# The prologue of a three-stage kernel laid out anew: loads four ahead, batch 0's attention beside the weight fold, block 0 fed from SBUF

## The chip, the cores and the metric

The kernel runs on one core of one Trainium2 chip. The metric is the device time of one execution in microseconds (us), from a few runs. A core has a matrix engine (TensorE, PE in the profile), a vector engine (VectorE, DVE), a scalar engine (ScalarE, ACT), GpSimd (POOL), and SyncE (SP), which here issues nearly all transfers. Each engine works through its own instructions in order and waits on semaphores that others raise. SBUF is the core's working memory, PSUM the memory that TensorE writes.

## The reference

Attention over keys and values that are averaged in groups of eight, then two feed-forward layers. B = 8 batches, H = 8 heads, S = 576 positions, D = 64, so 4608 tokens of 512 features. The second layer's inner width is 2048, the first's 1024.

```python
k_p = k.reshape(B, H, Sp, pool, D).mean(axis=3)
v_p = v.reshape(B, H, Sp, pool, D).mean(axis=3)
scores = scale * np.matmul(q, k_p.transpose(0, 1, 3, 2))
scores = scores - np.max(scores, axis=-1, keepdims=True)
attn = np.exp(scores)
attn = attn / (np.sum(attn, axis=-1, keepdims=True) + 1e-09)
attn_out = np.matmul(attn, v_p)
x = attn_out.transpose(0, 2, 1, 3).reshape(B * S, H * D)
x = ((x @ w1) * (x @ w2)) @ w3 @ w_out          # first layer
out = np.maximum(x @ w_in, 0.0) ** 2 @ w_out2   # second layer
```

The weights come as 64-bit floats, the rest as 32-bit floats.

## The kernel before, in words

Since `w3` and `w_out` of the first layer are multiplied with nothing between them, the kernel first makes W = w3 @ w_out (the **fold**), and then treats the tokens in nine **blocks** of 512. Block i needs a = x @ w1 and b = x @ w2 (`stage_ab`, eight steps u, 24 products of 128x512 each) and then (a*b) @ W (`stage_w`, 12 products a step, run two steps behind). So a block has 288 products, and 264 of block 0's fall before block 1 begins. After the blocks comes the second layer, which starts with the products of L965.

**Weights.** A weight tile of 128x512 arrives as 512 KB of raw 64-bit words. ScalarE makes two passes over it (`words`, L131 and L132) and VectorE three (`join`, L140, L141 and L143) to get 32-bit floats. Then w3 is turned on TensorE (L616) and copied back by ScalarE (L617), and w1 and w2 are split into a high part (ScalarE) and a low part (VectorE, L114), as each later product is made as high*high + high*low + low*high. The fold's own products are plain 32-bit ones (L641, two instructions each, 128 in all). There are 8 tiles of w_out, 16 of w3, 8 first halves of w1 and w2 (which stay in SBUF for `stage_ab`'s steps u < 4) and 8 second halves (steps u >= 4).

**Second halves.** `second_half` loads, converts and splits one of them, and stores its four pieces to DRAM (`store`, L207, 32 stores in all). Every block, block 0 too, fetches them again through a ring of eight buffers (`fetch`, L222; tiles `un`), two fetches for each w of each step u >= 4. Before step u = 3 of block 0 the kernel issues what is left of the second halves, then fills the ring. The quarter list (`make_quarters`: the second layer's weights, converted and stored to DRAM) starts only when the second halves are all issued, with one step of the list in three ticks.

**Attention.** `build_tasks` lists the attention of all batches as small tasks: transposes of k (`pe_kt`), scores with softmax (`pe_s`), transposes of the weights of attention (`pe_t`) and products with v (`pe_av`, which writes x, the block's input). A tick (`tick`) comes after each product of the fold, and after each six products of a block. Each tick adds `rate[0]` to a credit, and a whole credit runs a task: 0.7 a tick in the fold (from its twelfth product), 0.6 later. k and v are summed by VectorE from loads into `raw_p`, three buffers that the weights' raw tiles use too (`kv_parts`, L298). Once v is summed, `load_v` places it with 4 + 12 small transfers within SBUF (L333, L337). Block i waits until its tokens' `pe_av` are issued (`tokens_ready`): block 0 needs all of batch 0, block 1 all of batch 1.

**Order in the fold.** The first three w3 rows are folded together, with their first halves and the w_out tiles loaded into x's eight buffers (`x_p`), which stand empty then. All other raw tiles go through `raw_p`, each loaded just ahead of its conversion (`load64`, L125). From its fourth step on the attention starts: `load_k(0)`, `load_q(0, 0)`, and from the sixth `load_v(0)`. From its twelfth step on, a first half of w1 or w2 is converted at every fourth step (a step is one piece of 128 of the inner width, for all rows folded together).

## Time and profile before

| | us |
|---|---|
| median of 3 runs | 1585.99 |
| lowest, highest | 1585.23, 1586.9 |
| span of the profiled execution | 1583.2 |
| median above that span | 2.8 |

| engine | busy us in the span | share | instructions |
|---|---|---|---|
| PE | 1514.2 | 96% | 6944 |
| DVE | 992.7 | 63% | 1778 |
| ACT | 784.0 | 50% | 1905 |
| POOL | 83.9 | 5% | 146 |

The profile is of one execution; its own time beyond the span isn't listed, so the median stands for it. Busy time is the time with at least one instruction under way. PEclk is the granted TensorE clock as a share of full speed (2.4 GHz; the lower of its two levels, 1.2 GHz, is 0.5, and a stretch that has both shows a mean).

### The profile page before, as it was taken

The numbers are of one execution on the slowest core, as the hardware profiler recorded it, in microseconds if no ns is written. First come the engines' busy times: TensorE is split into PE (matmuls) and PEld (weight loads), VectorE is DVE, ScalarE is ACT, GpSimd is POOL, SyncE is SP. The second block draws the span as 40 slices with busy tenths as digits, with TensorE's granted clock in tenths as the row PEclk, the third lists the DMA queues.
The fourth block names the chain that finished last, engine by engine and source line by source line (L and its number), as shares of the span: only waits on it lengthen the run. The fifth ranks groups of instructions, "written<-read, shape, count | busy, mean of one in ns | idle before, by whom it ended". The sixth has DMA issues, their size and how long they took to land.

```text
span 1583.2 us, 21959 instructions
## 1 busy us (share of the span) xinstructions
PE 1514.2 (96%) x6944; PEld 1215.8 (77%) x6944; DVE 992.7 (63%) x1778; ACT 784.0 (50%) x1905; POOL 83.9 (5%) x146
## 2 busy tenths in 40 slices
PE   6788799998999999999999999999999999999998
PEld 3346577786868888887888887888788878888888
DVE  7688556675746667576435458648864877476542
ACT  6486544544425345555323565456445644464431
POOL 1111101110101010111000000000000000000000
PEclk8899799999989999999999999999999999999999
DMA  8455674756546676666727667677777766776774
GB/s 269 137 172 178 155 226 135 216 155 179 167 136 181 166 248 191 179 185 208 240 70 244 201 194 240 194 220 219 232 195 218 223 202 192 221 219 192 208 222 155
DMA packets 302930, 308.07 MB, mean 195 GB/s; under 512 B 131552, under 2 KB 188896, under 8 KB 302816
## 3 DMA queue, kind: packets, MB, share of 16 engines
q1 hardware_dynamic: 297632, 297.24, 64.4%
q10 hardware_dynamic: 5184, 9.44, 1.6%
q8 instruction: 56, 0.92, 0.2%
q14 instruction: 58, 0.48, 0.1%
HBM read 247.46 MB, written 56.62 MB: 192 GB/s over the span
## 4 chain that ended last, share of the span: by engine, by line
PE 78%; DVE 10%; DMA 4%; ACT 4%; SPq 3%; issue 2%; DVEq 0%; ACTq 0%
PE ps_w L183 23%; PE o L1052 14%; PE acc L183 11%; PE ps_a L965 5%; PE ps_c L965 5%; PE ps_d L965 5%; PE o L1112 3%; PE ps_h L183 3%; PE ps_b L965 2%; DVE gs L1030 2%; PE ps_s L414 2%; DVE gt L114 2%; PE ps_av L183 1%; DMA raw<-in_moe_w_dram 1%; PE ps_w L641 1%
## 5 line engine op out<-in xcount | busy, mean ns | idle before, releaser
L1052 PE MATMUL o<-gt,un 128*128 128x512 f32 x1344 | 330.8, 390 | 4.9 <-DVE gt L114 4.5
L1052 PEld LDWEIGHTS o<-gt,un 128*128 128x128 f32 x1344 | 251.3, 188 | 61.2 <-DVE gt L114 9.0
L114 DVE TENSOR_TENSOR gt<-gs,gt 128x512 fp32r<-128x512 f32 x240 | 163.8, 687 | 186.2 <-ACT gt L113 185.9
L113 ACT CAST gt<-gs 128x512 fp32r<-128x512 f32 x240 | 148.5, 619 | 164.0 <-PE o L1052 111.2
L183 PE MATMUL ps_w<-x,wt 128*128 128x512 f32 x864 | 221.6, 401 | 1.5 <-DVE x L495 0.8
L183 PE MATMUL acc<-gt,Wt 128*128 128x512 f32 x864 | 218.8, 396 | 0.0
L183 PE MATMUL ps_w<-x,un 128*128 128x512 f32 x864 | 216.2, 401 | 2.0 <-DVE x L495 1.5
L183 PEld LDWEIGHTS ps_w<-x,un 128*128 128x128 f32 x864 | 162.7, 192 | 36.1 <-DMA un<-u_w 2.0
L183 PEld LDWEIGHTS ps_w<-x,wt 128*128 128x128 f32 x864 | 157.9, 189 | 34.8 <-DVE x L495 2.1
L183 PEld LDWEIGHTS acc<-gt,Wt 128*128 128x128 f32 x864 | 158.2, 188 | 32.0 <-issue 1.0
L431 ACT ACTIVATE att<-ps_s,mx 128x72 f32<-128x72 f32 (+1 forms) x320 | 98.2, 320 | 76.6 <-DVE mx L429 70.3
L972 ACT ACTIVATE r<-r 128x512 f32<-128x512 f32 x96 | 60.5, 631 | 112.6 <-DVE r L1002 111.9
L965 PE MATMUL ps_c<-x2o,un 128*128 128x512 f32 x384 | 97.7, 390 | 0.0
L965 PE MATMUL ps_d<-x2o,un 128*128 128x512 f32 x384 | 97.4, 389 | 0.0
L965 PE MATMUL ps_a<-x2o,un 128*128 128x512 f32 x384 | 97.4, 389 | 0.0
L694 DVE TENSOR_TENSOR gf<-asb,ps_w 128x512 f32<-128x512 f32 x72 | 49.3, 685 | 71.3 <-PE ps_w L183 68.9
L973 ACT ACTIVATE gs<-r 128x512 f32<-128x512 f32 x144 | 89.5, 629 | 1.6
L1030 DVE TENSOR_TENSOR gs<-gs 128x512 f32<-128x512 f32 x128 | 83.6, 683 | 2.0 <-ACT gs L973 0.7
L690 ACT COPY asb<-ps_w 128x512 f32<-128x512 f32 x72 | 42.5, 590 | 84.6 <-PE ps_w L183 80.1
L965 PEld LDWEIGHTS ps_c<-x2o,un 128*128 128x128 f32 x384 | 71.9, 188 | 15.7 <-DVE u L996 0.9
L965 PEld LDWEIGHTS ps_d<-x2o,un 128*128 128x128 f32 x384 | 72.1, 188 | 15.0
L965 PEld LDWEIGHTS ps_a<-x2o,un 128*128 128x128 f32 x384 | 72.1, 188 | 15.0
(109 smaller groups left out, 1973.6 us busy)
## 6 DMA issues: line engine op xcount, KB each, us to landing
un<-u_w SPq DMA_DIRECT2D x144, 256.0 KB
un<-u_A SPq DMA_DIRECT2D x128, 256.0 KB
un<-u_S SPq DMA_DIRECT2D x128, 256.0 KB
un<-u_oA SPq DMA_DIRECT2D x128, 256.0 KB
un<-u_oS SPq DMA_DIRECT2D x128, 256.0 KB
raw<-in_moe_w_dram SPq DMA_DIRECT2D x32, 512.0 KB
raw<-in_moe_w_out_dram SPq DMA_DIRECT2D x24, 512.0 KB
x2d<-st ACTq DMA_DIRECT2D x36, 256.0 KB
```

The costliest lines, as they stand in the source:

```text
L113: nc.scalar.copy(hi, src)
L114: (eng or nc.vector).tensor_sub(lo, src, f32(hi))
L183: (lambda a=a, b=b, i=i: nc.tensor.matmul(ps, a, b, start=first and i == 0, stop=last and i == n - 1))
L431: nc.scalar.activation(av[:, h0 + h], sv[:, h], ACTF.Exp, bias=mx[:n, h:h + 1], scale=scale, accum_out=sm[:n, h0 + h:h0 + h + 1])
L690: nc.scalar.copy(asb, ps)
L694: nc.vector.tensor_mul(gf, asb, pss[1])
L965: nc.tensor.matmul(ps, l, r, start=first and j == 0, stop=j == len(todo) - 1, skip_group_check=True)
L972: nc.scalar.activation(t, src, ACTF.Relu)
L973: nc.scalar.activation(take(name), t, ACTF.Square)
L1030: nc.vector.tensor_sub(src, a, src)
L1052: nc.tensor.matmul(ob[x][o], l, r, start=u == 0 and m != 5 and j == 0, stop=u == NU - 1 and j == 2, skip_group_check=True)
L1112: nc.tensor.matmul(acc[o][:, y * PC:(y + 1) * PC], l, r, start=u == 0 and y == 0 and j == 0, stop=u == U2 - 1 and j == 2, skip_group_check ...
```

## The change

- A new pool `sec_p` (four tiles of 4 KB a partition) takes the place of the ring until block 0 has ended; the ring is then allocated where `sec_p` lay.
- The fold's conversions stand in one list, sorted by a position at which each begins: five positions ahead of its use at the latest, at least two apart (one apart ahead of the first product), w1's and w2's first halves at every sixth position from 14 on. Each conversion's passes stand at successive positions. At the pass `act` of conversion n the load of conversion n + 4 is issued (`PRE`), into `x_p` until the first x tile exists, then into `sec_p`.
- k of batch 0 is loaded first of all, into W's buffers, v's first three tiles too, and q of batch 0 into the buffers of w1 and w2; their sums and transposes become attention tasks. Batch 1's k and v loads are held until position 44.
- Credit per tick: 1.4 ahead of the first product, 0.85 from there, 0.5 from position 48, 0.7 in blocks 0 and 1, 0.6 later. The fold has 73 positions, with a tick each: six ahead of its first product, 64 with a product and three behind.
- `second_half` begins after the fold, one step a tick, w1 and w2 in turns. It writes to four tiles of `sec_p` and four of `prep_p`; block 0 reads them there. The 32 stores are still made, five ticks after the split, for blocks 1 to 8. The quarter list begins when the ring exists, after block 0.

```diff
 LEAD = 3
+
+PRE = 4
+
+W12_AT = 14
+
+W12_GAP = 6
 
 LAG = 2
...
-    ring = ctx.enter_context(tc.tile_pool(name="ring", bufs=RING))
     wW_p = tc.alloc_tile_pool(name="wW", bufs=U1)
     w0_p = tc.alloc_tile_pool(name="w0", bufs=2 * KD)
     prep_p = tc.alloc_tile_pool(name="prep", bufs=4)
+    sec_p = tc.alloc_tile_pool(name="sec", bufs=4)
     at_p = tc.alloc_tile_pool(name="att", bufs=1, side="right")
 
 
...
-            n_raw[0] += 1
-        r = pool.tile([P, TB, 2], U32, tag="x" if pool is x_p else "raw", name="raw")
+    def early_pool():
+
+        return sec_p if xt else x_p
+
+    def load64(src, pool):
+
+        tag = "x" if pool is x_p else "w" if pool is prep_p else "raw"
+        r = pool.tile([P, TB, 2], U32, tag=tag, name="raw")
         nc.sync.dma_start(r, src.bitcast(U32).rearrange("p (c t) -> p c t", t=2))
         return r
 
...
     n_used = [0]
...
             nc.sync.dma_start(f32(r), unit(key))
             ahead.append(r)
 
...
     def load_back():
-        if back["kv"] and (not held[0] or len(back["kv"]) > 9):
+        if back["kv"] and not wait_kv[0] and (not held[0] or len(back["kv"]) > 9):
             back["kv"].pop(0)[1]()
         if back["q"] and ticks[0] % 2 == 0:
             back["q"].pop(0)[1]()
...
-            raws[j] = r = raw_p.tile([P, POOL, D], F32, tag="raw", name="kv")
+            pool, tag = (raw_p, "raw") if b else (wW_p, "w")
+            raws[j] = r = pool.tile([P, POOL, D], F32, tag=tag, name="kv")
...
+        if b == 0:
+            fits = NJ if src is k else U1 - NJ
+            for j in range(fits):
+                load(j)
+            rest = [lambda: [load(j) for j in range(fits, NJ)]]
+            return rest + [(lambda j=j: total(j)) for j in range(NJ)] + last
         parts = [(lambda j=j: part(j)) for j in range(NJ + 2)] + last
         what = (src is k, b)
-        if b:
-            back["kv"].extend((what, fn) for fn in parts)
-        else:
-            for fn in parts:
-                fn()
+        back["kv"].extend((what, fn) for fn in parts)
...
+    q_nat = {}
+
+    def turn_q(b, hf, i):
+
+        if (b, hf) not in qts:
+            qts[b, hf] = at_p.tile([P, NP, HW], F32, tag="qT", name="qT", bufs=2)
+        t = qts[b, hf]
+        s0 = QT[HALF[hf][0]][0]
+        s1, n = QT[i]
+        r = q_nat.pop((b, i))
+        ps = ps_at.tile([P, NP, P], F32, tag="at", name="ps_q")
+        for hp in range(NP):
+            nc.tensor.transpose(
+                ps[:, hp, :n], r[:n, 2 * hp:2 * hp + 2, :].rearrange("p h d -> p (h d)"),
+                ident[:n, :n])
+        nc.scalar.copy(t[:, :, s1 - s0:s1 - s0 + n], ps[:, :, :n])
+
...
+        if b < EARLY:
+            for i in HALF[hf]:
+                s1, n = QT[i]
+                if b == 0:
+                    if i % 2 == 0:
+                        q_nat["w"] = w0_p.tile([P, 2, H, D], F32, tag="w", name="q_nat")
+                    r = q_nat["w"][:, i % 2]
+                else:
+                    r = tmp_p.tile([P, H, D], F32, tag="cg", name="q_nat", bufs=3)
+                nc.sync.dma_start(r[:n], q[b, :, s1:s1 + n, :].rearrange("h p d -> p h d"))
+                q_nat[b, i] = r
+            return
...
+                put(lambda part=part: pe_kt(b, part), [("k", b)])
...
+        def turns(g):
+            b, i = divmod(g, len(QT))
+            for hf, tiles in enumerate(HALF):
+                if b < EARLY and i == tiles[0]:
+                    for x in tiles:
+                        put(lambda hf=hf, x=x: turn_q(b, hf, x))
+
+        def ahead_of(g):
+            b, i = divmod(g, len(QT))
+            at = (len(QT) if b + 1 < EARLY else HALF[1][0], len(QT))
+            early = b + 1 < EARLY
+            if i + 1 == at[0] and b + 1 < B:
+                put(lambda b=b: load_q(b + 1, 0))
+            if i + 1 == at[1] and b + 1 < B:
+                if not early:
+                    put(lambda b=b: load_q(b + 1, 1))
+                kt(b + 1)
+            if g + 1 < NG:
+                turns(g + 1)
+                sc(g + 1)
+            if i + 1 == at[1] and early:
+                put(lambda b=b: load_q(b + 1, 1))
...
+        for fn in first_k:
+            put(fn)
         kt(0)
+        turns(0)
         sc(0)
-        put(lambda: load_q(0, 1))
...
+            if g + 1 != len(QT):
+                ahead_of(g)
...
+            if g == 0:
+                for fn in first_v:
+                    put(fn)
...
+            if g + 1 == len(QT):
+                ahead_of(g)
...
+        mms = [(m, f) for m in range(nm) for f in range(LEAD)]
+        mms += [(m, f) for f in range(LEAD, U1) for m in range(nm)]
+        use = {}
+        for pos, (m, f) in enumerate(mms):
+            use.setdefault(("w3", f, m // nh), pos)
+            use.setdefault(("wo", m), pos)
+        begin = {}
+        nxt = len(mms)
+        for key, pos in sorted(use.items(), key=lambda z: -z[1]):
+            begin[key] = nxt = min(pos - 5, nxt - (2 if nxt > 1 else 1))
+        w12 = [("w12", n, kc) for kc in range(KD) for n in range(2)]
+        for j, key in enumerate(w12):
+            begin[key] = W12_AT + W12_GAP * j
+        convs = sorted(begin, key=lambda key: begin[key])
+        raws = {}
+        n_load = [0]
...
+                raws[key] = load64(src, early_pool())
+
+        def conv(n, key):
+            st = {}
+
+            def act():
+                load(n + PRE)
+                if key[0] == "w3":
...
+            steps = [act, lambda: join(raws.pop(key), st["w"])]
+            steps += {"w3": [turn, copy], "wo": [], "w12": [hi, lo]}[key[0]]
+            for x, fn in enumerate(steps):
+                put(begin[key] + x, fn)
+
+        for n, key in enumerate(convs):
+            conv(n, key)
...
+        for f in range(U1):
+            end = max(pos for pos, mf in enumerate(mms) if mf[1] == f)
+            put(end + 3, lambda f=f: merged(f))
+        first_k = load_k(0)
+        load(2)
+        load_q(0, 0)
+        load(5)
+        first_v = load_v(0)
+        load_q(0, 1)
+        tasks.extend(build_tasks(first_k, first_v))
+        rate[0] = 1.4
+        for pos in range(min(at), max(at) + 1):
+            if pos == 0:
+                rate[0] = 0.85
+            if pos == 44:
+                wait_kv[0] = False
+            if pos == 48:
+                rate[0] = 0.5
+            for fn in at.get(pos, []):
+                fn()
+            if 0 <= pos < len(mms):
+                m, f = mms[pos]
+                if m == 0:
+                    acc_w[f] = ps_acc.tile([P, TB], F32, tag="acc", name="ps_w")
+                nc.tensor.matmul(
+                    acc_w[f], w3t[f][:, m, :], wo_t[m // 2][:, m % 2, :],
+                    start=m == 0, stop=m == nm - 1)
+            tick()
+        assert n_load[0] == len(convs)
 
...
-        if (i, u) == (0, TB // P - 1):
-            until(lambda: not fh1)
+        if (i, u) == (1, 0):
             for _ in range(RING):
                 fetch()
...
-            if fh:
+            if fh and i:
...
-                ws = [(wt[nm_, kc, 0][:, 0, cs], wt[nm_, kc, 0][:, 1, cs]) for kc in range(KD)]
+                ws = [(wt[nm_, kc, fh][:, 0, cs], wt[nm_, kc, fh][:, 1, cs]) for kc in range(KD)]
...
-    def start_attention():
-        load_k(0)
-        load_q(0, 0)
-        tasks.extend(build_tasks())
-        rate[0] = 0.7
-
-    def second_half(nm_, w, kc):
+    def second_half(x, nm_, w, kc):
...
-            st_["t"] = t = st_["r"].bitcast(F32R).rearrange("p c t -> p (c t)").rearrange(
-                "p (y c) -> p y c", y=2)
+            pool, tag = (sec_p, "raw") if x < 4 else (prep_p, "w")
+            wt[nm_, kc, 1] = t = pool.tile([P, 2, TB], F32R, tag=tag, name="wt2")
             nc.scalar.copy(t[:, 0, :], st_["w"])
...
         def put():
             for u in range(TB // P, U1):
-                store(st_["t"], (u - TB // P) * P, (nm_, u, kc // 2), kc % 2)
-            done.add((nm_, kc, 1))
-
-        return [(0, load), (2, act), (3, lambda: join(st_["r"], st_["w"])), (4, hi), (5, lo), (6, put)]
-
-    fh1 = merge([second_half(nm_, w, kc) for nm_, w in (("w1", w1), ("w2", w2))
-                 for kc in range(KD)], 2)
+                store(wt[nm_, kc, 1], (u - TB // P) * P, (nm_, u, kc // 2), kc % 2)
+
+        return [(0, load), (3, act), (4, lambda: join(st_["r"], st_["w"])), (5, hi), (6, lo), (11, put)]
+
+    fh1 = merge([second_half(2 * kc + x, nm_, w, kc) for kc in range(KD)
+                 for x, (nm_, w) in enumerate((("w1", w1), ("w2", w2)))], 2)
+
     def feed_w12():
-        if fh1 and (folded or ticks[0] % 2 == 0):
+        if fh1 and folded:
             run_step(fh1)
...
     folded.append(True)
+    pumps.append(feed_w12)
     until(lambda: tokens_ready(TB))
-    rate[0] = 0.6
...
-        if not fh1 and quarters and not operands and ticks[0] % rate_q[0] == 0:
+        if ring and quarters and not operands and ticks[0] % rate_q[0] == 0:
...
-    for i in range(NB):
+    for i in range(1, NB):
...
+        if i == 1:
+            rate[0] = 0.6
+        if i == 0:
+            until(lambda: not fh1)
+            sec_p.release()
+            ring.append(tc.alloc_tile_pool(name="ring", bufs=RING, reuse_waits="tile"))
```

## Rows read from the trace of the kernel before

**Rows 1.** The page, busy tenths of 40 equal slices.

```profile
PE   6788799998999999999999999999999999999998
...
PEclk8899799999989999999999999999999999999999
```

**Rows 2.** Engines by stretch of the span; columns in the first line.

```profile
core 0: us, PE busy (x) PEld busy (x) DVE busy (x) ACT busy (x) POOL busy (x), PEclk, DMA share, GB/s
0.00:130.50 130.50, 97.52 (x344) 53.00 (x344) 97.53 (x185) 83.26 (x227) 16.82 (x32) 0.91 0.61 190
11.00:60.00 49.00, 38.06 (x121) 21.09 (x122) 41.20 (x73) 28.16 (x77) 3.58 (x8) 0.83 0.73 225
60.00:80.00 20.00, 15.27 (x53) 7.84 (x51) 9.06 (x19) 10.30 (x31) 1.60 (x3) 0.93 0.33 101
80.00:130.50 50.50, 43.10 (x168) 23.35 (x167) 43.83 (x88) 39.33 (x114) 8.77 (x12) 0.96 0.57 174
130.50:180.00 49.50, 45.79 (x217) 37.20 (x216) 36.83 (x75) 26.91 (x79) 4.54 (x9) 0.97 0.56 162
130.50:228.20 97.70, 84.01 (x376) 67.39 (x376) 62.12 (x132) 48.73 (x155) 8.40 (x16) 0.88 0.69 195
180.00:201.00 21.00, 11.02 (x44) 7.66 (x43) 10.26 (x28) 11.90 (x52) 3.23 (x6) 0.58 0.76 208
228.20:311.60 83.40, 82.04 (x395) 64.75 (x393) 56.43 (x115) 40.22 (x139) 10.69 (x20) 1.00 0.59 166
```

**Rows 3.** TensorE in order of time: block 0 begins, stops, resumes; block 1 begins.

```profile
130.54 0.73 PE L183 MATMUL ps_w<-x,wt 128*128 128x512 f32 x2
...
167.92 2.88 PE L183 MATMUL ps_w<-x,un 128*128 128x512 f32 x12
...
200.90 15.14 PE L183 MATMUL ps_w<-x,un 128*128 128x512 f32 x60
...
228.24 1.09 PE L183 MATMUL ps_w<-x,wt 128*128 128x512 f32 x4
```

**Rows 4.** The chain of waits, 160 to 201 us.

```profile
162.77 0.94 SPq L333
...
166.46 0.61 SPq L337
...
178.13 4.25 DMA raw<-in_moe_w_dram
...
184.29 1.92 DMA u_w<-raw
```

**Rows 5.** The DMA queue SP in order of time: start, issue time, transfer.

```profile
4.76 2.88 SPq L288 DMA_DIRECT2D kv<-in_k_dram  x3
...
56.85 3.87 SPq L333 DMA_DIRECT2D vl<-vhl  x4
60.82 7.96 SPq L337 DMA_DIRECT2D vr<-vhl  x12
...
69.47 37.33 SPq L125 DMA_DIRECT2D raw<-in_moe_w_dram  x13
```

**Rows 6.** VectorE's groups by line, 0 to 130.5 us.

```profile
L141 DVE SCALAR_TENSOR_TENSOR raw<-raw 128x512 uint32<-128x512 uint32 x32 | 22.0, 687 | 0.5
```

**Rows 7.** The chain of waits: TensorE at full granted clock.

```profile
66.02 0.44 PE ps_w L616 x4
...
85.11 1.72 PE ps_w L641 x4
...
239.34 5.46 PE ps_w L183 x24
```

**Rows 8.** VectorE's first work, in order of time.

```profile
5.86 0.43 DVE L140 TENSOR_SCALAR raw<-raw 128x512 uint32<-128x512 uint32 x1 [5.86 <-ACT w L132]
```

**Rows 9.** Second weights' converted quarters; first product that reads them.

```profile
L826 SPq DMA_DIRECT2D u_oS<-oq x32: 513/611/1637, 598.2 to 857.4; - x32
...
L965 PE MATMUL ps_a<-x2o,un x384: 388/389/389, 865.7 to 1405.2; 128*128 128x512 f32 x192
```

More of the change, by code (lines that the diff above doesn't have):

```diff
@@ L164, in run_step @@
             fn()
-    def load_split(pool, src, key, eng=None):
-        r = load64(src)
-        t = pool.tile([P, 2, TB], F32R, tag="w", name="wt")
-        w = tmp_p.tile([P, TB], F32, tag="cg", name="w32", bufs=3)
-        to32(r, w)
-        split(t[:, 0, :], t[:, 1, :], w, eng)
-        done.add(key)
-        return t
     def mm3(ps, pairs, first=True, last=True):
@@ L209, in store @@
             stored.add(key)
+    ring = []
     useq = []
@@ L220, in fetch @@
                 run_step(quarters)
-            r = ring.tile([P, 2, 2, P], F32R, tag="unit", name="un")
+            r = ring[0].tile([P, 2, 2, P], F32R, tag="unit", name="un")
             nc.sync.dma_start(f32(r), unit(key))
@@ L319, in copies @@
             nc.gpsimd.tensor_copy(kp[:JL, NJ - 1, 1, :], kp[:JL, NJ - 1, 0, :])
-        kv_parts(k, b, lambda j: kp[:, j, 0, :], [copies])
+            done.add(("k", b))
+        return kv_parts(k, b, lambda j: kp[:, j, 0, :], [copies])
     def load_v(b):
@@ L339, in place @@
             done.add(("v", b))
[L341 removed]
+        return kv_parts(v, b, lambda j: vp[:, j, :], [cut, place])
     def pe_kt(b, part):
@@ L517, in kt @@
             for part in range(2):
-                put(lambda part=part: pe_kt(b, part))
+                put(lambda part=part: pe_kt(b, part), [("k", b)])
         def sc(g):
@@ L659, in fold, with put @@
-        assert not w12
+        at = {}
+        def put(pos, fn):
+            at.setdefault(pos, []).append(fn)
+        mms = [(m, f) for m in range(nm) for f in range(LEAD)]
[8 more added lines that the diff above has]
+            begin[key] = nxt = min(pos - 5, nxt - (2 if nxt > 1 else 1))
@@ new lines, in fold, with merged @@
+        for n, key in enumerate(convs):
+            conv(n, key)
+        def merged(f):
+            t = wW_p.tile([P, 2, TB], F32R, tag="w", name="Wt")
+            wt["W", f] = t
+            split(t[:, 0, :], t[:, 1, :], acc_w[f])
+            done.add(("W", f))
+        for f in range(U1):
[5 more added lines that the diff above has]
+        load(5)
@@ L1174, in attn_moe_moe2_kernel @@
     folded.append(True)
+    pumps.append(feed_w12)
     until(lambda: tokens_ready(TB))
-    rate[0] = 0.6
-    feeds = []
-    second = []
+    rate[0] = 0.7
+    late = []
     def feed_quarters():
-        if not fh1 and quarters and not operands and ticks[0] % rate_q[0] == 0:
+        if ring and quarters and not operands and ticks[0] % rate_q[0] == 0:
             run_step(quarters)
@@ L1189, in begin_second @@
     def begin_second():
-        if tasks or second:
+        if tasks or late:
             return
         at_p.release()
-        second.append(tc.alloc_tile_pool(name="gs", bufs=1, side="right", reuse_waits="tile"))
+        late.append(tc.alloc_tile_pool(name="gs", bufs=1, side="right", reuse_waits="tile"))
         for x in range(20):
-            slots.append(second[0].tile([P, TB], F32, tag=f"gs{x}", name="gs"))
+            slots.append(late[0].tile([P, TB], F32, tag=f"gs{x}", name="gs"))
     operands = []
@@ L1238, in attn_moe_moe2_kernel @@
         f()
-    until(lambda: second)
+    until(lambda: late)
     order = iter(order)
@@ L1300, in attn_moe_moe2_kernel @@
             (o_step if step[0] == "o" else po_step)(*step[1:])
-    for p in reversed(second):
+    for p in reversed(late):
         p.release()
-    for p in (prep_p, w0_p, wW_p):
+    for p in (ring[0], prep_p, w0_p, wW_p):
         p.release()
```

132 lines of the change are left out of this document (46 added, 86 removed).

## The prediction

> **What bounds the kernel now.** I read the page's slices first: TensorE is full nearly everywhere, and the lean stretch is the first eighth of the span, where the granted clock dips too [rows 1]. Then the stretches, for what TensorE lacks [rows 2]. The fold, 0 to 130.5 us, has it busy for 97.5 us at a granted clock of 0.91; VectorE is busy just as long, 97.5 us, and ScalarE 83.3. Block 0, 130.5 to 228.2, takes 97.7 us, and block 1 83.4, at full clock and with TensorE busy for 82.0 of it. So what the change can win lies ahead of 228 us; behind it 1583.2 - 228.2 = 1355.0 us follow whose work stays.
>
> Two places stand out. From 60 to 80 us VectorE is busy for only 9.1 of 20 us: the SP queue spends 56.9 to 68.8 on placing v, 16 issues one after the other, and the next raw weight is issued at 69.5 [rows 2, 5]. From 180 to 201 TensorE is busy for 11.0 of 21 us at a granted clock of 0.58: it has the first of block 0's products with fetched weights at 167.9, and the next at 200.9 [rows 2, 3]. The chain between them runs through SP (16 placements from 162.8 on), a raw weight's load (178.1, 4.25 us), and a store of 1.9 us [rows 4]: weights go out to DRAM and back behind a busy queue.
>
> **The change part by part.** All is made against the span of 1583.2; the median of the runs is 2.8 above it, and I add that back.
>
> *Counts.* 32 raw tiles are converted in the fold before [rows 6] and after, eight more for the second halves, with the same passes. Attention's work is moved, not cut; its POOL instructions (16.8 us of 130.5 [rows 2]) keep their order. What is removed is block 0's 16 fetches, and from SP's path in front of u = 4 the stores and fetches. I cost these instructions at nothing: they were transfers behind a queue, and the wait that they caused is counted below.
>
> *The start.* k's five loads now stand ahead of the first weight on SP. Three such issues took 2.9 us [rows 5], so five take some 4.8, against the 1.3 to 2.1 us of a few weights: VectorE's first pass, at 5.9 us [rows 8], comes at some 8.5. The fold's first product then waits for six conversions, and the third for the loads ahead of wo's third tile (some 6.3 MB; 225 GB/s at a DMA share of 0.73 from 11 to 60 us [rows 2] makes 308 GB/s when all are busy, 20 us) and for its conversion, so I put the start of steady products at 24 us.
>
> *TensorE in the fold.* 128 product instructions at 1.72/4 = 0.43 us are 55.0 us; 64 transposes at 0.44/4 = 0.11 are 7.0 [rows 7]; a batch's attention is what block 1 holds besides 288 products at 5.46/24 = 0.2275: 82.0 - 65.5 = 16.5 [rows 2, 7]. Sum 78.5 at full clock, 86 at the granted 0.91. From 24 us that ends at 110. Block 0's first four steps (96 products and 24 of `stage_w`, 27.3 us, with 20 of 48 ticks of attention, 6.9) end at 144. So TensorE alone could be at u = 4 by 144 us.
>
> Here a rule speaks against the change. The row is 0.83 granted from 11 to 60 us, where TensorE had pauses, and 1.00 in block 1, where it had almost none [rows 2]. The Trainium skill (TensorE: Matmul & The Clock Gate, section HAM oscillation — how this bites in real kernels) says that a stream with pauses falls back to the half clock and starts each burst cold. The new fold spreads its products among conversions, so it has many pauses. By the row the fold's TensorE work costs 86 us, by the rule in the extreme, all at half clock, 157. The rows of 180 to 201, with 0.58, agree that it happens; how far is a rival below.
>
> *VectorE.* It sets the pace. Before block 0's u = 4 it must have done what it did in the kernel before by about 180 us: 97.5 + 36.8 = 134.4 us [rows 2], plus some 2.5 for the last second half, less some 3 for tasks of batch 1 that fall later: 134 us of work. How densely can it be fed? As now from its first pass to 130.5: 97.5 / 124.6 = 0.78. In the fold's later part 43.8 / 50.5 = 0.87; from 11 to 60, 0.84. The upper end is where TensorE takes over. I take 0.87: that stretch was not blocked by a placement, and loads four ahead keep the 12 us of SP's placements covered by four conversions, which is what the 60 to 80 hole was. Then u = 4 can start at 8.5 + 134 / 0.87 = 162.5 us. With 0.78 it is 180; with 1.0 it would be 142.5, below TensorE's 144. ScalarE has less to do (83.3 against 97.5) and runs on the same inputs; it doesn't come first.
>
> *Block 0's second part.* Steps 4 to 7 are 96 products and 48 of `stage_w`, 32.8 us, with half of a batch's attention, 8.3: 41 us. The second halves are in SBUF by then, 21 ticks after the fold; so u = 4 waits for VectorE and not for a fetch. Block 1 starts at 162.5 + 41 = 203.5. Its start may need a few ticks more until batch 1's tokens are issued (the tasks are some two short of the credit given): 1.5 us. 205 against 228.2: 23 us.
>
> *What moves behind it.* The quarter list starts half a block later, some 24 ticks or 8 of its steps. It was over at 857 us, when the first product of the second layer came at 866 [rows 9]; 8 steps that now fall among that layer's first products, one a group of six products (1.4 us), end some 45 groups ahead of the first that reads them (56 groups stand ahead of the products with the output weights). Cost nothing, hidden by those groups; without that cover 8 steps times about 1.5 us of VectorE, 12 us. The ring's first eight fetches are issued at the start of block 1 and wait for block 0's last reads; four steps of some 9 us cover them. The rate of 0.7 in block 1 moves some five tasks forward; nothing to gain or lose in sum. I take 0 for all of this, bounds -4 and +4 us.
>
> Sum: 1583.2 - 23 = 1560.2, plus 2.8: **1563 us**.
>
> **The rivals.**
> - *VectorE is fed no better than now* (0.78): u = 4 at 180, block 1 at 223, 5 us won: 1581. For it: VectorE's passes alternate with ScalarE's and TensorE's in fixed orders, and attention's chains now stand between all of them. Against: the largest hole has a cause that the loads ahead remove.
> - *VectorE is fed almost fully* (0.95): u = 4 at 149.5, block 1 at 192, 36 us won: 1550. For it: nothing else is then late. Against: no stretch of the prologue shows it.
> - *The second halves come late anyway*: eight loads of 4.25 us through three buffers, behind stores and batch 1's loads on SP. In the kernel before, the last was loaded at 178 to 182, some 50 us behind the fold's end, and used 10 us later. If 60 us remain, from a fold that ends at 128 (162.5 less the 34 of the four steps), u = 4 starts at 188 and block 1 at 230.5: 1588, no change that can be told. Against: stores come five ticks behind the split now, and no load waits for them.
> - *The clock* (the other side): the fold at 0.58 throughout, as from 180 to 201, takes 78.5 / 0.58 = 135 us from 24 on; it ends at 159, u = 4 at 193, block 1 at 235.5: 7 us lost, 1593. It decides from where the fold ends behind 151 us, that is below a granted 78.5 / 127 = 0.62. Against: 0.83 to 0.96 in all stretches of the fold before, with TensorE busy for 75% of it; after, 78.5 of some 102 us.
>
> **How the numbers follow.** My forecast gets 0.65; VectorE fed as now 0.13; fed almost fully 0.10; second halves late 0.06; the clock 0.06. The predicted time is the first's. Its own span is set by 0.83 to 0.92 (u = 4 at 170 to 154, block 1 at 212 to 196, with the 4 us of the rest): 1551 to 1574. The range of 1548 to 1581 takes in VectorE fed as now and fed almost fully, the neighbours on both sides, in part, and leaves out the late halves and the clock. A measurement of this kernel tells about 0.2%, 3.2 us, from no change. Faster: 0.65 + 0.13 + 0.10 = 0.88; within: 0.05; slower: 0.07, the clock and a little of the late halves.
>
> **What would show it.** Right: VectorE over 0.85 busy from 20 to 120 us, with no hole of 20 us; no raw load issued over 10 us behind its turn; the first product with SBUF-held second halves at 155 to 170 us with no pause of several us ahead of it; block 1's first product at 196 to 212; as much time from there to the end as before, within 4 us. Wrong: a granted clock under 0.7 in the fold; ScalarE or VectorE waiting for raw loads again; a pause ahead of u = 4; or a second layer that starts later than 638 us behind block 1's start, which is what it took before (866 - 228).

## The result and the profile after

| | before | after |
|---|---|---|
| median of 4 runs, us | 1585.76 | 1550.43 |
| lowest, highest, us | 1585.23, 1586.9 | 1549.5, 1552.07 |
| ratio, 95% interval | | 0.9781 [0.9767, 0.9795] |
| span of the profiled execution, us | 1583.2 | 1547.7 |

The kernel is 35.3 us faster, 12 us more than forecast, inside the range and near its lower end, just below the 1551 to 1574 us that I gave the forecast itself. Line numbers below are those of the kernel after. The slices of the page answer to [rows 1]: the lean eighth has shrunk to its first two slices, and no slice of the clock falls below 9.

```profile
PE   5799999999999999999999999999999999999998
...
PEclk9999999999999999999999999999999999999999
```

The stretches answer to [rows 2] and have its columns: the fold, two parts of it, block 0 up to u = 4, and block 0 as far as block 1's first product.

```profile
0.00:117.00 117.00, 91.01 (x340) 50.24 (x341) 100.44 (x193) 79.23 (x211) 13.83 (x29) 0.97 0.67 211
60.00:80.00 20.00, 15.17 (x58) 9.18 (x57) 15.07 (x32) 14.51 (x37) 0.00 (x0) 0.83 0.70 251
80.00:117.00 37.00, 35.12 (x138) 18.77 (x137) 36.03 (x69) 22.97 (x66) 4.94 (x8) 1.00 0.56 159
117.00:153.50 36.50, 34.07 (x171) 27.43 (x170) 26.93 (x57) 25.47 (x82) 6.24 (x11) 1.00 0.54 149
117.00:197.30 80.30, 77.22 (x381) 61.57 (x379) 55.14 (x114) 46.12 (x159) 12.37 (x22) 1.00 0.59 157
```

The fold takes 117.0 us instead of 130.5. From 60 to 80 us VectorE is busy for 15.1 of 20 us where it was busy for 9.1, and behind 80 us for 36.0 of 37. By 50 us it has begun 15 conversions in both kernels; by 80 us 19 before and 25 after. From 117 on it is no longer the busy one: 26.9 of 36.5, and TensorE 34.1. Block 0 takes 80.3 us instead of 97.7. The stretch from 60 to 80 still has a hole, and a dip of the clock behind it:

```profile
60.00:67.40 7.40, 4.91 (x19) 2.44 (x17) 3.32 (x6) 2.42 (x5) 0.00 (x0) 1.00 0.48 164
67.40:74.20 6.80, 4.66 (x14) 3.35 (x15) 6.12 (x13) 6.28 (x14) 0.00 (x0) 0.50 0.98 346
```

TensorE in order of time, from the fold's first run of steady products on, answers to [rows 3]:

```profile
31.95 5.42 PE L754 MATMUL ps_w<-wo,w3t 128*128 128x512 f32 x12 [0.80 <-DVE wo L148]
...
69.54 0.80 PE L178 MATMUL ps_av<-aT,vl 128*128 128x256 f32 x2 [4.32 <-DVE x L513]
...
117.00 1.65 PE L178 MATMUL ps_w<-x,wt 128*128 128x512 f32 x6
...
153.52 1.55 PE L178 MATMUL ps_w<-x,wt 128*128 128x512 f32 x6
...
197.35 1.04 PE L178 MATMUL ps_w<-x,wt 128*128 128x512 f32 x3
```

Ahead of the row at 69.54 TensorE stands idle for 4.3 us; in that time the granted clock falls to its lower level, and it is back at 74.2. The row at 153.52 is the first product with second halves: no wait stands on it, and its operand is `wt`, in SBUF. SP in order of time answers to [rows 5]:

```profile
0.74 2.46 SPq L286 DMA_DIRECT2D kv<-in_k_dram  x5
...
50.72 3.94 SPq L334 DMA_DIRECT2D vl<-vhl  x4
54.77 7.56 SPq L338 DMA_DIRECT2D vr<-vhl  x12
62.43 4.82 SPq L130 DMA_DIRECT2D raw<-in_moe_w_dram  x8
...
156.17 15.34 SPq L202 DMA_DIRECT2D u_w<-wt  x24
```

The 16 placements still take 11.6 us in a row, and weights still follow behind them. k's five issues take 2.5 us, where I had put 4.8 from the three of 2.9. 24 of the 32 stores come behind u = 4's first product. VectorE's first work answers to [rows 8]: k's sums at 3.6 us, and the first pass over a weight at 10.0.

```profile
3.61 1.93 DVE L296 TENSOR_REDUCE kp<-kv 128x64 f32<-128x512 f32 x2 [3.61 <-DMA kv<-in_k_dram]
...
10.03 0.43 DVE L145 TENSOR_SCALAR raw<-raw 128x512 uint32<-128x512 uint32 x1 [0.87 <-ACT wo L137]
...
191.03 0.69 DVE L791 TENSOR_TENSOR gf<-asb,ps_w 128x512 f32<-128x512 f32 x1 [0.77 <-PE ps_w L178]
...
827.91 0.68 DVE L791 TENSOR_TENSOR gf<-asb,ps_w 128x512 f32<-128x512 f32 x1
```

Its last two rows are marks that I cut all runs at: the product a*b of the eighth step of block 0, and the same of block 8. In the kernel before they stand here:

```profile
224.24 0.69 DVE L694 TENSOR_TENSOR gf<-asb,ps_w 128x512 f32<-128x512 f32 x1 [1.19 <-PE ps_w L183]
...
863.81 0.68 DVE L694 TENSOR_TENSOR gf<-asb,ps_w 128x512 f32<-128x512 f32 x1
```

So the **head** (to the first mark) is shorter by 33.2 us, the **blocks** (between the marks) by 2.7 (639.6, 636.9), and the rest of the span is 0.4 longer (719.4, 719.8). The sum, 35.5, is the difference of the spans.

The quarter list ends at 838.1, with the second layer's first product at 827.7, and the first fetch that reads it comes at 913.4 (before: [rows 9]).

```profile
L218 SPq DMA_DIRECT2D un<-u_oS x128: 319/320/1713, 913.4 to 1470.0; - x128
L923 SPq DMA_DIRECT2D u_oS<-oq x32: 512/578/1835, 614.2 to 838.1; - x32
```

Why VectorE's hole went can be read from the waits in the fold (columns: who waited for whom, us in total, times, longest). Before:

```profile
DVE raw L140 <- ACT w L132: 14.0, 9, 5.9
...
ACT raw L131 <- DMA raw<-in_moe_w_dram: 15.4, 9, 5.8
```

After:

```profile
ACT raw L136 <- DMA raw<-in_moe_w_out_dram: 6.7, 1, 6.7
...
ACT raw L136 <- DMA raw<-in_moe_w_dram: 4.2, 5, 1.6
...
DVE raw L145 <- ACT w L137: 1.7, 2, 1.4
```

Raw weights came late to ScalarE for 15.4 us, and what ScalarE was late with, VectorE lacked for 14.0. After, both are small; the one wait of 6.7 us is for the first tile of `w_out`, at the start, where VectorE has k's sums to make. And why weights came late is in the waits of SP from 69 to 107 us in the kernel before:

```profile
SPq L125 <- DVE w L143: 28.1, 10, 4.7
```

Ten raw loads waited for VectorE's last pass over an earlier tile, that is, for a free buffer. The eight of the changed kernel at 62 us waited for nothing longer than 0.3 us.

### The profile page after: what moved, and what is told of

The parts are those of the page before. It is cut to its first block, busy times and chain, and to the rows that moved or that the text cites. A ratio compares the mean times of both kernels' runs of the same rounds, so it can differ in the third digit from the quotient of the medians.

```text
span 1547.7 us, 21838 instructions
## 1 busy us (share of the span) xinstructions
PE 1498.4 (97%) x6944; PEld 1204.2 (78%) x6944; DVE 989.7 (64%) x1778; ACT 780.7 (50%) x1905; POOL 82.1 (5%) x146
## 4 chain that ended last, share of the span: by engine, by line
PE 73%; DVE 12%; DMA 5%; ACT 4%; SPq 3%; issue 2%; DVEq 0%; ACTq 0%
PE ps_w L178 21%; PE o L1149 15%; PE acc L178 10%; PE ps_c L1062 5%; PE ps_d L1062 5%; PE ps_a L1062 5%; PE o L1209 3%; PE ps_h L178 3%; PE ps_b L1062 2%; DVE gs L1127 2%; PE ps_s L432 2%; DVE gt L120 2%; SPq L338 2%; DMA raw<-in_moe_w_dram 1%; PE ps_av L178 1%
## 5 line engine op out<-in xcount | busy, mean ns | idle before, releaser
L178 PE MATMUL ps_w<-x,wt 128*128 128x512 f32 x960 | 249.9, 401 | 2.2 <-DVE x L513 1.1
L178 PEld LDWEIGHTS ps_w<-x,wt 128*128 128x128 f32 x960 | 174.2, 189 | 39.1 <-DVE x L513 3.0
L178 PE MATMUL ps_w<-x,un 128*128 128x512 f32 x768 | 191.1, 396 | 2.1 <-DMA un<-u_w 2.1
L178 PEld LDWEIGHTS acc<-gt,Wt 128*128 128x128 f32 x864 | 158.8, 189 | 34.1 <-ACT st L819 1.8
L178 PEld LDWEIGHTS ps_w<-x,un 128*128 128x128 f32 x768 | 140.8, 188 | 30.8 <-ACT oq L872 1.8
L1062 PE MATMUL ps_a<-x2o,un 128*128 128x512 f32 x384 | 97.7, 390 | 1.6 <-ACT r L1069 1.6
L1062 PE MATMUL ps_d<-x2o,un 128*128 128x512 f32 x384 | 97.5, 389 | 0.0
L119 ACT CAST gt<-gf 128x512 fp32r<-128x512 f32 x72 | 44.8, 623 | 81.7 <-DVE gf L791 77.6
```

Of the source, the lines that this page charges most:

```text
L119: nc.scalar.copy(hi, src)
L178: (lambda a=a, b=b, i=i: nc.tensor.matmul(ps, a, b, start=first and i == 0, stop=last and i == n - 1))
L1062: nc.tensor.matmul(ps, l, r, start=first and j == 0, stop=j == len(todo) - 1, skip_group_check=True)
```

## The experiments

Each was run with the kernel before on the same chip (1584.9 to 1585.8 us). "Fold" is the time of the first product of block 0. The marks are those above.

| run | median, us | ratio [95%] | fold | head | blocks |
|---|---|---|---|---|---|
| after | 1550.43 | 0.9781 [0.9767, 0.9795] | 117.0 | 191.0 | 636.9 |
| after, again | 1551.27 | 0.9787 [0.9771, 0.9802] | 120.0 | 194.5 | 637.5 |
| loads at their own turn | 1552.74 | 0.9793 [0.9773, 0.9812] | 116.8 | 192.0 | 638.1 |
| three raw buffers | 1578.9 | 0.9957 [0.9936, 0.9978] | 126.9 | 208.5 | 648.6 |
| block 0 through DRAM | 1578.61 | 0.9951 [0.9934, 0.9969] | 117.6 | 208.5 | 644.3 |
| before, block 0 from SBUF | 1567.85 | 0.9886 [0.9868, 0.9903] | 131.4 | 207.4 | 640.0 |
| k and q behind five weights | 1555.88 | 0.9809 [0.9791, 0.9827] | 122.7 | 198.6 | 636.3 |
| VectorE pass twice | 1564.92 | 0.9871 [0.9856, 0.9886] | 127.3 | 202.4 | 639.9 |
| ScalarE pass twice | 1556.95 | 0.9824 [0.9806, 0.9841] | 118.7 | 193.3 | 640.7 |
| rate 0.6 from block 1 | 1544.99 | 0.9751 [0.9733, 0.9769] | 119.1 | 194.9 | 628.9 |
| the same, again | 1545.94 | 0.975 [0.9732, 0.9768] | 117.5 | 191.3 | 630.0 |
| placements on GpSimd | 1562.47 | 0.9864 [0.9845, 0.9883] | 113.6 | 189.5 | 646.4 |
| rate 0.6, batch 0's on GpSimd | 1545.14 | 0.9751 [0.9729, 0.9773] | 111.5 | 187.1 | 635.0 |

The two rows of the changed kernel show what one profiled execution is worth: its fold and head differ by 3.0 and 3.5 us, its blocks by 0.6. A smaller difference in a column proves nothing.

**Theory and rival.** The theory: VectorE sets the fold, and gains because weights are issued four conversions ahead of their use; block 0 gains because its weights don't go through DRAM. The rivals: the order on SP is not what counts but the buffers; ScalarE or TensorE sets the fold; one of the two parts does all.

**Loads at their own turn.** A load stands at its own conversion's turn on SP, the loads ahead of the first turn excepted.

```diff
-PRE = 4
+PRE = 1
```

> The changed kernel with loads one ahead in place of four (PRE = 1). If loads ahead feed VectorE and so shorten the fold (my reason): the fold ends 8 to 15 us later than the changed kernel's 117.0 us, VectorE is busy for less than 0.80 of it, 1558 to 1566 us in all. If the fold is shorter because attention stands beside it from the start and the loads are early enough anyway: the fold ends within 3 us of 117, 1549 to 1553 us.

Nothing is lost: the fold ends at 116.8 us, with VectorE busy for 97.4 of them. The theory as I put it falls, and the other reading holds. (`load(upto)` stops short of `upto`, so with `PRE = 4` it is conversion n + 3's load that is issued at conversion n, and with 1 its own.)

**Three raw buffers.** All raw tiles of the fold go through `raw_p`'s three buffers, which k and v of batch 1 use too.

```diff
-PRE = 4
+PRE = 1
...
-        return sec_p if xt else x_p
+        return raw_p
...
-        load(5)
+        load(3)
```

> The changed kernel with all the fold's raw weights loaded into the three buffers that k and v of batch 1 use too, each load at its own conversion. Since one load ahead in place of several changed nothing, the buffers are what is left of the loads: if SP runs ahead by itself as far as free buffers go, and three are too few: VectorE has a hole of 8 us or more behind the placements, the fold ends 5 to 10 us later, 1556 to 1562 us. If the loads don't matter at all, and the fold is shorter for k's early sums and the spread alone: within 3 us, 1549 to 1553 us.

On TensorE, in order of time:

```profile
126.88 2.05 PE L178 MATMUL ps_w<-x,wt 128*128 128x512 f32 x4
128.73 4.05 PE L754 MATMUL ps_w<-wo,w3t 128*128 128x512 f32 x8
```

Four of block 0's product instructions come ahead of the fold's last eight here, so the table's 126.9 is not the fold's end: its last product ends at 132.8. That is 13 to 16 us later than in the changed kernel (116.8, 119.8 in the repetition), and no earlier than in the kernel before (128.2), with the same list and the same rates. On SP, in order of time, and SP's wait in that stretch:

```profile
59.54 29.10 SPq L130 DMA_DIRECT2D raw<-in_moe_w_dram  x11
```

```profile
SPq L130 <- DVE w L148: 22.4, 9, 4.4
```

Eleven raw loads spread over 29.1 us on SP, nine of them waiting for VectorE to free a buffer, as 13 were spread over 37.3 in the kernel before [rows 5]; in the changed kernel eight went out in 4.8 us. Here is ScalarE's wait for them in the fold:

```profile
ACT raw L136 <- DMA raw<-in_moe_w_dram: 12.8, 10, 3.4
```

So without the added places for raw tiles nothing is left of the fold's gain, while the turn at which a load is issued changed nothing. That the places alone would bring the gain is not shown: the kernel before was not run with more buffers, and this run has fewer at the start than that kernel, which loads into x's eight there too. Two of my figures missed: VectorE has no hole of 8 us (it is busy for 16.4 of 20 us from 60 to 80), its waits are spread; and the time lies 17 us above the expected range, as the blocks take 11.1 to 11.8 us more too. Why they do is open.

**VectorE pass twice.** In each of the fold's 32 conversions the shift pass is made a second time ahead of the passes, with the same result: it reads only the high words, and the first time has not changed them.

```diff
-            steps = [act, lambda: join(raws.pop(key), st["w"])]
+            def again():
+                r = raws.pop(key)
+                lo, hi_ = (r[:, :, i].rearrange("p (y c) -> p y c", y=2) for i in range(2))
+                nc.vector.tensor_scalar(lo, hi_, 3, None, op0=ALU.logical_shift_left)
+                join(r, st["w"])
+
+            steps = [act, again]
```

> The changed kernel with one VectorE pass of each of the fold's 32 conversions (the shift) made twice, with the same result: 32 x about 0.40 us = 13 us more VectorE work. If VectorE's work sets the fold's length: the fold ends 9 to 14 us later than 117.0, 1559 to 1565 us in all. If the chain between the engines, the loads or TensorE set it: within 4 us of 117, 1550 to 1554 us.

**ScalarE pass twice.** The second pass of `words` is repeated in each of them.

```diff
                 words(raws[key], st["w"])
+                nc.scalar.activation(
+                    st["w"].bitcast(U32), raws[key][:, :, 0], ACTF.Copy, scale=2.0 ** -29)
```

> The changed kernel with one ScalarE pass of each of the fold's 32 conversions made twice, with the same result: 32 x about 0.56 us = 18 us more ScalarE work (79 of 117 us busy now). If VectorE's work sets the fold: it ends 0 to 6 us later, 1550 to 1557 us. If the chain of passes in fixed order sets it, ScalarE as much as VectorE: 10 to 18 us later, 1560 to 1569 us.

The fold of the one and then of the other, by engine:

```profile
0.00:127.30 127.30, 97.36 (x339) 53.01 (x340) 109.75 (x222) 79.48 (x214) 17.51 (x29) 0.93 0.61 194
```

```profile
0.00:118.70 118.70, 92.60 (x341) 50.37 (x341) 98.94 (x191) 96.83 (x246) 13.88 (x29) 0.97 0.66 208
```

VectorE's 9.3 us more of busy time lengthen the fold by 10.3 against one run of the changed kernel and 7.3 against the other (a little of it may be TensorE's, at 0.93 of the clock in place of 0.97). ScalarE's 17.6 us lengthen it by no more than those two differ (1.7 longer, 1.3 shorter). VectorE sets the fold; ScalarE has some 18 us to spare there. No run adds work to TensorE alone, which is busy for 35.1 of the fold's last 37 us: how much more it could take is open. The whole time still rises by about 6 us, 3.2 to 3.8 of it in the blocks; why a pass that ends with the fold costs time behind it is open.

**Block 0 through DRAM again.** The changed kernel, but second halves split in place, stored and fetched by block 0 through the ring, which stands from the fold's end on; the quarter list begins once they are all issued, as in the kernel before.

```diff
-        if (i, u) == (1, 0):
+        if (i, u) == (0, TB // P - 1):
+            until(lambda: not fh1)
             for _ in range(RING):
                 fetch()
...
-            if fh and i:
+            if fh:
...
-    for i in range(1, NB):
+    for i in range(NB):
```

> The changed kernel with block 0's second halves stored to DRAM and fetched again, as in the kernel before; fold and rates as changed. If the trip through DRAM made block 0 long (my reason): a pause of over 8 us ahead of u = 4 with a granted clock under 0.8, block 0 at 92 to 98 us in place of 80.3, 1561 to 1568 us. If block 0 is shorter because batch 1's attention and the second halves are better spread (rates, order) and the trip is hidden by the first four steps: block 0 within 3 us of 80.3, 1550 to 1554 us.

The pause is back: from 163.7 to 176.7 us TensorE makes no product of block 0, only small pieces of attention with waits between them. Then, in order of time on TensorE:

```profile
176.74 2.77 PE L178 MATMUL ps_w<-x,un 128*128 128x512 f32 x6
181.47 4.22 PE L178 MATMUL ps_w<-x,un 128*128 128x512 f32 x12 [1.97 <-DMA un<-u_w]
```

From 165 to 190 us TensorE is busy for 16.6 of 25 us at a granted clock of 0.73:

```profile
165.00:190.00 25.00, 16.56 (x61) 12.18 (x62) 13.08 (x30) 12.24 (x39) 3.23 (x6) 0.73 0.80 243
```

Block 0 takes 93.8 us, as expected with the trip. The head is 17.4 us longer than after's, 13.9 than its repetition's. The blocks take 7.4 more; one wait of TensorE for a fetched weight, 6.8 us, stands among them, where the changed kernel's longest is 1.4. What delayed that fetch is open. The time lies 10.6 us above the expected range, and the blocks' 7.4 are part of that.

**The kernel before, with block 0 from SBUF.** The other way round: only `sec_p`, the late ring and `second_half` after the fold.

```diff
+            pool, tag = (sec_p, "raw") if x < 4 else (prep_p, "w")
+            wt[nm_, kc, 1] = t = pool.tile([P, 2, TB], F32R, tag=tag, name="wt2")
...
-        if (i, u) == (0, TB // P - 1):
-            until(lambda: not fh1)
+        if (i, u) == (1, 0):
...
-            if fh:
+            if fh and i:
...
+    pumps.append(feed_w12)
```

> The kernel before with the block 0 part alone: second halves begun after the fold, one step a tick, kept in SBUF, the ring allocated after block 0; fold, loads and rates as before. If the parts add up and the trip through DRAM is worth what block 0 gained: the fold ends at about 130, block 0 takes 80 to 87 us, 1566 to 1575 us. If block 0 needs the new rates and the shorter fold as well: block 0 over 92 us, 1580 us or more.

```profile
131.40:207.40 76.00, 71.50 (x341) 56.73 (x341) 52.06 (x108) 39.54 (x125) 7.82 (x14) 1.00 0.57 154
```

The fold stays at 131.4, block 0's clock is whole, and the head is 16.9 us shorter than before. The new fold without this part (the run through DRAM) is 15.8 shorter. 32.7 together, against 33.2 for the whole change: in the head the parts add, about half each, and fold, block 0 (83.5 us) and time are as expected for that.

**k and q behind five weights.**

```diff
+        load(5)
         first_k = load_k(0)
-        load(2)
         load_q(0, 0)
-        load(5)
```

> The changed kernel with batch 0's five k loads and two q loads issued behind the first five weights. If VectorE's work sets the fold and k's sums fill its wait for the first weights: VectorE starts at about 6 us in place of 3.6 and the fold ends 2 to 6 us later, 1552 to 1557 us. If the first weights' arrival sets the fold (products start earlier with weights first): the fold ends 2 to 4 us earlier, 1546 to 1549 us.

VectorE makes its first pass at 5.6 us, as in the kernel before, but from 20 to 40 us it is busy for only 13.6 of 20, at a granted clock of 0.77, where the changed kernel has 17.3 and 1.00:

```profile
20.00:40.00 20.00, 14.96 (x49) 8.39 (x48) 13.56 (x29) 13.90 (x48) 4.10 (x6) 0.77 0.78 264
```

```profile
20.00:40.00 20.00, 16.71 (x70) 9.35 (x70) 17.33 (x39) 15.70 (x50) 3.23 (x6) 1.00 0.91 308
```

The fold ends 2.7 to 5.7 us later, the time is 4.6 to 5.5 longer. k's loads ahead cost no time, as I had charged them; they earn some.

**Rate 0.6 from block 1 on**, instead of from block 2.

```diff
-        if i == 1:
-            rate[0] = 0.6
...
         if i == 0:
+            rate[0] = 0.6
             until(lambda: not fh1)
```

> The changed kernel with the rate 0.6 from block 1 on, as before, in place of 0.7 in block 1; block 0 as changed. If the rate is what made blocks 1 to 3 shorter (83.4 + 90.3 + 88.3 = 262.0 before, 81.3 + 82.9 + 84.3 = 248.5 changed): they take 5 us more at least, 1555 to 1560 us. If the rate does nothing and they are shorter for the later quarter list or the fold's end state: within 2 us, 1549 to 1552 us.

> The changed kernel with the rate 0.6 from block 1 on, once more. If the higher rate in block 1 costs time (1545.0 us at first): 3 to 8 us below the changed kernel of this call. If that was scatter between executions: within 2 us of it.

> The changed kernel once more, beside the others of this call: 1549 to 1552 us, with the fold's end at 117 to 119 us and the eighth product pair of block 0 at 190 to 195.

What I expected of the first of these fell, in both readings: from block 1's first product to block 4's the time stays as it was (248.5 us in the changed kernel, 249.3 and 248.1 with the lower rate), and the rate does count, later. The second run came as its first reading says; the repetition of the changed kernel at 1551.27, with its fold at 120.0, 1 us past what I gave. The lower rate makes the kernel shorter, by 5.4 and 5.3 us, against the changed kernel in the first and in the repeated pair. The blocks take 628.9 and 630.0 instead of 636.9 and 637.5. TensorE's idle time in them (length less busy time) is 5.2 and 4.8 us instead of 9.6 and 11.3. The remaining 0.9 to 3.6 us are a shorter busy time. From 400 to 720 us, in the changed kernel and then with the lower rate:

```profile
400.00:720.00 320.00, 313.30 (x1491) 252.75 (x1491) 202.51 (x420) 157.45 (x499) 31.73 (x54) 0.99 0.67 198
```

```profile
400.00:720.00 320.00, 318.71 (x1533) 257.79 (x1533) 204.75 (x425) 157.94 (x506) 33.66 (x55) 1.00 0.65 191
```

The changed kernel's waits here are single ones of 0.2 to 1.4 us, on fetched weights, on VectorE, on ScalarE and on placements of v, from two blocks behind the one whose rate is changed. That tasks pulled forward in block 1 shift how later tasks meet the products is my reading of it, not shown.

**Placements on GpSimd's queue**, for all batches.

```diff
-            nc.sync.dma_start(f32(vl)
+            nc.gpsimd.dma_start(f32(vl)
...
-                    nc.sync.dma_start(f32(vr)
+                    nc.gpsimd.dma_start(f32(vr)
```

> The changed kernel with v's 16 placement transfers issued by GpSimd's queue in place of SP's, in all batches. If SP's 12 us of placements cost what follows them (a raw load issued late at 62 us, fetches late in block 4): VectorE's hole at 62 to 68 us closes, the fold ends 2 to 5 us earlier, 1541 to 1548 us. If GpSimd's issues delay its own softmax work or the transfers themselves come later: 1552 us or more.

SP's 11.6 us in front of the weights go: VectorE is busy for 18.3 us from 60 to 80, and the fold is 3.4 to 6.4 us shorter, as expected. But the time is 11 to 12 us longer: the blocks lose 9 us, though the profiled execution is the fastest of its runs (1556.93). In them TensorE waits for placements of v for 7.1 us, in two waits; in the changed kernel for 0.4. The chain of waits shows the longer one:

```profile
602.12 0.52 POOL vl L334
602.64 0.29 issue
602.92 7.10 DMA vl<-vhl
...
610.16 0.77 PE ps_av L178 x2
```

The placement is issued as soon as v's sum is there, and takes 7.1 us to land. The same place in the changed kernel, on SP and then on TensorE:

```profile
600.36 3.65 SPq L334 DMA_DIRECT2D vl<-vhl  x4
```

```profile
603.79 0.48 PE L178 MATMUL ps_av<-aT,vl 128*128 128x256 f32 x2 [0.36 <-DMA vl<-vhl]
```

From SP's first issue to the product 3.4 us pass, from GpSimd's 8.0. So the transfer is late, by some 4.6 us, and not for GpSimd's other work ahead of it. That GpSimd's issue makes it slow is not shown. SP, which has no placements to issue now, sends stores and two raw weights meanwhile, which in the changed kernel come behind the placements, at 611 and 613 us. Here is the stretch from 602 to 610 us in this run and then in the changed kernel:

```profile
602.00:610.00 8.00, 3.14 (x14) 2.25 (x12) 1.51 (x3) 1.27 (x2) 5.28 (x9) 0.97 1.02 303
```

```profile
602.00:610.00 8.00, 7.52 (x39) 5.54 (x38) 2.18 (x7) 3.66 (x16) 1.15 (x1) 1.00 0.35 102
```

The DMA engines are full in the one, at a share of 1.02, and at 0.35 in the other. At 293 to 298 us of this run, where the share is 0.54, four placements from GpSimd land in 2.0 to 2.7 us. The Trainium skill (DMA: Bandwidth & Descriptors, section Issuing engine by pattern) calls transfers issued from SyncE generally faster than those from GpSimd; these rows can't tell that from the other transfers' load. The two waits make most of the blocks' loss, 6.7 of 9 us; the rest is open.

**Rate 0.6 and batch 0's placements alone on GpSimd.**

```diff
         def place():
+            eng = nc.sync if b else nc.gpsimd
...
-            nc.sync.dma_start(f32(vl)
+            eng.dma_start(f32(vl)
```

(the same for `vr`, on top of the lower rate)

> The rate 0.6 from block 1 on, and batch 0's placements alone on GpSimd's queue. The fold ended 3.4 us earlier with all placements there, and what came later was longer. If both add up: 1540 to 1545 us, the fold's end at 113 to 115 us. If the gain in the fold is given back behind it: 1544 to 1549 us.

The fold is the shortest of all, 111.5 us, and the time is that of the lower rate alone. Against it the head gains 4.2 and 7.9 us, and the blocks lose 5.0 and 6.1. A shorter fold wasn't kept here, as the second of my expectations has it. Some 4 us of it go in block 1 alone (86.0 us to block 2's first product, 81.8 and 82.0 with the lower rate alone); by which chain is open. The lower rate alone (0.9751 and 0.975) is as good as any version found.

## Why the prediction was right, and where it was off

1. *The gain lies ahead of block 1, and its size comes from two places.* Right: 33.2 of 35.5 us are in the head, split about evenly between fold and block 0's second halves. By block 1's first product, which I had forecast 23 us earlier, it is 30.9 (228.24 to 197.35).
2. *Loads four ahead cover the placements.* There is a cover, but the named cause is wrong, and it isn't whole. With loads at their own turn nothing changes; with three buffers the gain of the fold is gone. What the fold's gain needs is places for raw tiles. And from 60.0 to 67.4 us, behind the placements, VectorE is busy for only 3.3 of 7.4 us; without them on SP the fold is 3.4 us shorter at least.
3. *VectorE sets the pace: right for the fold, wrong for u = 4.* This is the term that was mis-sized. I put 134 us of work at a density of 0.87 behind 8.5 us, and got 162.5. Measured: 127.4 us of VectorE's work by u = 4 (100.4 and 26.9), at 153.5. In the fold the density from its first work at 3.6 us is 100.4 / 113.4 = 0.89, close to my 0.87. But from the fold's end on VectorE had slack (26.9 of 36.5) and TensorE had little (34.1 of 36.5). By my own split the fold should have ended at 128; it ended at 117, and block 0's first four steps then took 36.5, where I had 34. I had charged VectorE, ahead of u = 4, with all work that it did before 180 us in the old kernel. Of the 9.0 us by which u = 4 came earlier than 162.5, VectorE's earlier start (3.6 for 8.5) gives 4.9 and its smaller work 7.6; its density over the whole, 127.4 / 149.9 = 0.85, takes 3.5 back.
4. *The start.* k's loads delay the first weight pass to 10.0, a little more than I said (8.5), but VectorE works on k's sums from 3.6 on, so the delay costs nothing. Steady products came at 32 us, not at 24, and TensorE's work in the fold took 91.0 us of busy time, where I had 78.5 at full clock. It didn't matter: VectorE set the fold.
5. *The clock.* I gave its rival 0.06, and nothing to its opposite. The rival fell: the fold's granted clock is 0.97 where it was 0.91, block 0's 1.00 where it was 0.88. With nearly the same instructions (340 and 381 records, before 344 and 376) TensorE is busy for 91.0 and 77.2 us instead of 97.5 and 84.0. In block 0 that 6.8 us counts, as TensorE sets it; together with 10.6 us less of idle time (13.7 to 3.1) it is the 17.4 by which block 0 is shorter. The Trainium skill (TensorE: Matmul & The Clock Gate, section HAM oscillation — how this bites in real kernels) says that a stream of products with pauses for transfers falls to the half clock and starts again cold. The 0.73 of the run through DRAM, around its pause, agrees, and so does the 0.50 from 67.4 to 74.2 us in the changed kernel's fold, though the wait of 4.3 us in which it begins is one for VectorE. From 80 us to the fold's end the clock is 1.00. One of this rival's figures was wrong beside the chance: with my other terms the clock would set the pace from a fold that ends behind 128 us on, not 151; at 151 the whole gain is gone.
6. *Block 0's second part.* 41 us from u = 4 to block 1, and 1.5 for tokens: 42.5. Measured 153.5 to 197.35, 43.8.
7. *Behind the head nothing: 0 ± 4.* By the marks 2.7 gained and 0.4 lost, within the bounds; from block 1's first product to the end 4.7 gained (1355.0 to 1350.3), just over them, and 3.5 in the repetition, within them. That it comes out so small is luck in part. From block 1's first product to block 4's the time fell from 261.9 to 248.5 us (the granted clock is 1.00 in place of 0.97, TensorE's idle time 3.6 us in place of 10.6), and from there to the second mark it rose from 373.7 to 382.1. I had foreseen neither. The runs with one half of the change alone have the first gain too (248.4 us with block 0 from SBUF, 247.9 through DRAM); why is open. The list's end behind the second layer's first products cost nothing, 75 us ahead of the first fetch that needed it. (The products of the second row of [rows 9] are the layer's first; those that read the list's last pieces come later.) But "the rate of 0.7 in block 1, nothing to gain or lose" was wrong by 5 us, which the lower rate gives: with it the second of these parts takes 373.3 and 375.6 us.
8. *Late second halves* fell: u = 4 waited for none. *Fed as now* fell. *Fed almost fully* had the closest time (1550) with block 1 at 192 and the wrong reason: the fold's VectorE was at 0.89, and what came out better was u = 4's bound.
9. *The signs.* VectorE was busy for 0.90 of 20 to 120 us, block 1 began at 197.35, both as said. The first product with second halves at 153.5 came just ahead of my 155 to 170 (157.0 in the repetition). The second layer began 630 us behind block 1, not later than 638. Of the signs against, ScalarE's wait for raw tiles stayed in part.

## What to carry to other kernels

Where an engine waits for loads, ask first which buffer the next load would land in and who still reads it, and only then in what place of the program it is issued; a second run with the buffers taken away tells. Where a transfer is late, look at what else the DMA engines carry before its queue is blamed. When a stretch is bounded by an engine's work, count the work that must be done by that point in the new order, not what happened to be done by then in the old one. A saving in a prologue is worth what is left at the last block's mark: two of the shorter folds here were given back in the blocks.

## What the runs showed that I had not expected

- Issuing the fold's raw loads at their own turn, three conversions later, cost nothing (116.8 against 117.0 and 120.0 us of fold); taking the added raw buffers away cost 13 to 16 us.
- A task rate raised for one block of nine cost 5 us, most of it in idle time of TensorE spread over later blocks.
- A placement of v issued from GpSimd took 7.1 us to land with the DMA engines full (a share of 1.02), and 2.0 to 2.7 us at 0.54. With placements on SP, SP's own other transfers wait behind them, and the share was 0.35.
- TensorE's work in fold and block 0 takes 13.3 us less busy time, at granted clocks of 0.97 and 1.00 instead of 0.91 and 0.88.
